# A fused retention and Fourier-mixing kernel: new turns for the work between batch 0's feed-forward products, and two filler matmuls moved to the head

## The chip, the cores and the metric

The kernel runs on one core of one Trainium2 chip. The metric is the device time of one execution in microseconds (us). Its engines are TensorE (PE in the profile; PEld is its loading of weights), VectorE (DVE), ScalarE (ACT), GpSimd (POOL) and SyncE (SP), which here only issues DMAs. Each works through its own queue in the order in which the program was written out for it.

## The reference, cut to what matters

Inputs are q, k and v of 4 batches, 8 heads, 768 positions and 64 channels, and two weights, w1 (512 x 2048) and w2 (2048 x 512). Per head, a decaying state is carried over the positions, then the heads are put side by side to x of 768 x 512 per batch:

```python
state = gamma * state + outer(k[t], v[t])
y[t] = (q[t] @ state) / sqrt(64)
```

Then x is mixed by a two-dimensional Fourier transform (over positions and channels) of which the real part is kept, added to itself, normalised per row, and sent through a feed-forward net:

```python
u = x + real(fft(fft(x, axis=1), axis=2))
un = (u - mean(u)) / sqrt(var(u) + 1e-6)
out = u + relu(un @ w1) @ w2
```

## The kernel before, in words

**Stages of a batch.** *Attention* goes by pairs of heads, four pairs a batch, in 6 chunks of 128 positions. `cast_unit` turns the loaded q, k and v into f16 on POOL (k scaled by powers of gamma), `t_unit` transposes q and k (batches 0 and 1 on PE, line 610, later ones by DMA), `a_unit` makes the products within a chunk (line 654) and masks them on DVE, `kv_unit` makes the states (line 673) and sums them over chunks on ACT and DVE, `y_unit` makes y from states and products (lines 704 and 708), which ACT scales into x (line 716). *Folding* (`fold_s`, `fold_d`, `fold_e`, DVE) uses the symmetries of the transform. *Stage one* (`s1_unit`, line 837) and *stage two* (`s2_unit`, from line 980) are the two transforms as products with tables. Stage two gives one block of 128 rows at a time: blocks 0 to 2 directly, blocks 3 to 5 as *mirror rows* from the reversed result of stage one. After the matmuls (lines 999, 1015, 1018) come copies on ACT, two sums on DVE, two sums with x on POOL (1027, 1029), statistics on DVE (1040, 1041), and on ACT `un`, the centred rows in f16 (1042). `unT_unit` transposes such a block (PE, line 1065, and a copy; from batch 1's block 3 on by DMA). The pool of `un` has two buffers. *Feed-forward*: the rows are in two halves of three blocks. The first product (`h_unit`, line 1078, 16 units of 4 matmuls; for batch 0's first half `h0_unit`, line 1095, 4 units of 16 small matmuls for each block) goes through relu on ACT or DVE (1082, 1084; 1102, 1104) into `ht16`. The second product (`ch_unit`, line 1121) takes a block of rows in four quarters of four matmuls; DVE adds u after the fourth (1125), and SP writes the block out (1129). PSUM, the matmuls' output memory, holds 5 buffers in the pool for attention and transforms, and 3 in the pool for the feed-forward.

**The head.** Batch 0's attention and transform are written out by hand in the text `FIRST`: each name is a unit, `@v`, `@a`, `@g` its engine, and `pin` fixes that order on every engine. It also has the eight weight loads `w0` to `w7` (POOL, lines 1135 and 1142), one each for a fourth of w1 and of w2. A *filler* is a 128x512 matmul of zeros (line 167) whose result is not used; `filler(6)()` at line 235 issues six before all else, and `fill1` in `FIRST` issues one.

**Turns.** After the head, everything is placed by due times. The feed-forward units of a batch are the *majors*: 56 units of batch 0 are due at 1/56, 2/56, ... 1.0. Here the 16th is a square root for the norm, the 17th to 28th are the quarters of the first half's second product, then 16 units of the first product of the second half, and so on. Every other list of units is a stream with a start and an end, and its units are due at even steps between them (`emit`, line 1238):

```python
for i, u in enumerate(units):
    ev.append((t0 + (t1 - t0) * (i + 1.0) / len(units), si, i, u))
ev.sort(key=lambda e: e[:3])
```

The units are written in that order. A scheduler at compile time then lays out each engine's queue: it takes earlier turns first, by its own estimates of durations, and lets a later turn go ahead where an earlier one has to wait for an operand or a buffer. On POOL, and for turns below 0.05 on every engine, the written order is fixed up to turn 1.0.

The constants for batch 0 and its border with batch 1 are: `DM0`, start and end of its mirror rows and of their transposes; `TS0`, start and end of batch 1's first cast and then the bounds of its five further steps of attention; `DA0`, counted from the end of `TS0`, start and end of batch 1's stage one, of its stage two for blocks 0 to 2, and of these blocks' transposes; `LD0`, the loads of batch 1, which wait for the seventh weight load (`w6`) and for the last first product of block 1; `HT0`, two units on DVE, `half_tables` (tables for stage two of batches 1 to 3) and `pad_unit` (zeros). `DM1`, `TS1`, `DA1` and `LD1` are the same for later batches.

Of the kernel before, what the change touches and what calls it, by code (L numbers as in the profile page):

```python
# [36 lines left out]
ae001@v kv0 ae000@v ae011@v t10 sc0 t11 e10@a yi01 v10@g yi00 yx0 e11@a am10 q2 x01@a am11 ts3  # L37
ta32 ta20 x00@v ta01 fl4@g ae101@v ae100@v k21@a kv1 t20 ta21 e20@a ae111@v yi11 t21 sc1
ae110@v yi10 fs0 fl2@g yx1 q3 s110 k31@g e21@a x10@v am20 am21 x11@a fs1 ta40 v22@a s010 k30@a
t30 e30@a fill1 t31 v21@g e31@a ae201@v ta30 ae200@v kv2 ae211@v yi21 ae210@v gk2@g sc2 csn2@a  # L40
w0 w1 csn1@v fill1 am30 ae300@v ta31 yi20 yx2 v32@g x20@a ae301@v xs0@v x21@a ta41 fl3@a gk3@g
s100 am31 ae311@v s000 v31@g kv3 fs2 s101 ge10@a ae310@v w2 s001 w3 yi31 sc3 ge00@a yi30 yx3 g0
x30@a sa00 sa10 edge x31@v fs3 w4 gr0 sa11 csn0@v s011 xs2@a xs3@v w5 s111 xs1@a sa20 mean
ge01@a sa02 sa01 ge11@v sa03 nh0@a gr3 sa12 nh1@a gr1 sa13 g1 sa21 pt0 g2 ua1@v pt1 sa22 pe0@a
# [1 line left out]
"""  # L46
ON_ACT = {'q': (0, 1, 0), 'kv': (1, 1, 1), 'g': (0, 1, 1), 'gr': (0, 0, 0)}
FB = 1
DM0, DM1 = (0.121, 0.179, 0.253, 0.368), (0.004, 0.137, 0.232, 0.341)
TS0 = (0.269, 0.376, 0.393, 0.441, 0.517, 0.575, 0.665, 0.696)  # L50
TS1 = (-0.040, -0.020, 0.048, 0.585)
DA0, DA1 = (0.034, 0.100, 0.173, 0.180, 0.306, 0.315), (0.063, 0.067, 0.063, 0.158, 0.168, 0.189)
LD0, LD1 = (0.160, 0.263), (-0.370, 0.140)
HT0 = (0.683, 0.767, 0.685, 0.583)
NPE = 2
ACT_ROWS = ((2, 5, 6, 7, 8, 9, 10, 14), (0, 3, 6, 7, 9, 10, 11, 12, 14, 15), (2, 4, 5, 6, 7, 8, 10, 14))

# [2 lines left out]
def kernel(  # L60
# [48 lines left out]
    gk2 = const.tile([P, NHP], f32, tag="gk2")  # L109
# [54 lines left out]
    def filler(n):  # L164
        def run():
            for _ in range(n):
                nc.tensor.matmul(wps, wz[:, 0:P], wz, start=True, stop=True)
        return run
# [63 lines left out]
    nc.gpsimd.iota(icol_i[:, 5:6], pattern=[[0, 1]], base=127, channel_multiplier=-1)  # L232
    nc.gpsimd.iota(kf_i, pattern=[[1, KN]], base=0, channel_multiplier=0)
    nc.gpsimd.memset(wz, 0.0)
    filler(6)()
    for h in range(H):
        nc.vector.memset(lgrow[:, h:h + 1], float(lng[h]))
    nc.vector.memset(maskf, 1.0)
# [1020 lines left out]
    for b in range(B):  # L1259
# [17 lines left out]
        if b + 1 < B:  # L1277
            steps = attn_steps(b + 1)
            if b == 0:
                streams.append(([load_unit(1, i, 6) for i in range(4)], LD0[0], LD0[1]))  # L1280
                streams.append(([qt_zeros], 0.1, 0.15))
                streams.append(([half_tables], HT0[0], HT0[1]))
                streams.append(([pad_unit], HT0[2], HT0[3]))
                ts = TS0
            else:
# [42 lines left out]
```

## Time and profile before

| what | us |
|---|---|
| time, median of 3 runs | 245.77 (245.33 to 245.82) |
| the profiled execution's own time | 246.28 |
| its span, first to last instruction | 244.1 |
| PE busy in the span | 231.0 |
| DVE busy | 173.6 |
| ACT busy | 121.3 |
| POOL busy | 83.5 |

The profile is of one execution. Its rows give starts in us from the span's start. A busy matmul row is longer than the time by which the next one follows, as matmuls overlap: a quarter's four 128x512 matmuls follow each other every 0.216 us, so that a quarter takes 0.86 us, and this is how the chain of waits counts them. In the chain, each row is what the next one waited for, in order of time; "issue" is time in which nothing that the profile shows was waited for. A row of the waits says: engine and line, who ended the wait, total us, how many waits. SPq and POOLq are the sequencers of SP and POOL, which issue DMAs. The batches' places in the span are: head to 33 us, batch 0's feed-forward from there to 94 us, then some 52 us for each of the others.

### The profile page before, as it was taken

What the parts mean: (1) busy time and instruction counts of PE and PEld (TensorE: products, weight loads), DVE (VectorE), ACT (ScalarE), POOL (GpSimd) and SP (SyncE); (2) the same over time, 40 slices, a digit from 0 to 9 for tenths busy, and PEclk for the clock granted to TensorE, in tenths of its full rate; (3) what the DMA queues carried; (4) which work ended last, traced back from release to release, by engine and by line L of the source; (5) the groups of instructions that cost most, each with busy time, mean ns of one, the idle gap of its engine ahead of it and who ended that gap; (6) DMA issues with size and microseconds to landing.
All of it is one profiled execution on the core that took longest, in us unless ns stands there. A gap on an engine that the chain in (4) does not pass through costs nothing.

```text
span 244.1 us, 5274 instructions
## 1 busy us (share of the span) xinstructions
PE 231.0 (95%) x2010; PEld 144.6 (59%) x2010; DVE 173.6 (71%) x423; ACT 121.3 (50%) x268; POOL 83.5 (34%) x151
## 2 busy tenths in 40 slices
PE   4499999997999998999999999999999999999995
PEld 1376779755775645665567446665666455445543
DVE  8879987947887788995985748887895556424112
ACT  5989758755785434842247515732257317202500
POOL 7578802456500067690000736660002305000000
PEclk9999999999999999999999999999999999999999
DMA  7997999999999388999999478585100441221012
GB/s 176 232 271 104 199 201 203 221 245 260 268 237 216 69 172 190 182 187 139 262 269 217 92 161 196 118 143 134 72 0 0 46 150 23 43 89 43 1 43 89
DMA packets 99209, 36.39 MB, mean 149 GB/s; under 512 B 89840, under 2 KB 96240, under 8 KB 99184
## 3 DMA queue, kind: packets, MB, share of 16 engines
q1 hardware_dynamic: 94960, 31.86, 63.2%
q0 software_dynamic: 4224, 4.19, 10.8%
q8 instruction: 16, 0.26, 0.5%
q14 instruction: 9, 0.07, 0.1%
HBM read 27.26 MB, written 6.29 MB: 137 GB/s over the span
## 4 chain that ended last, share of the span: by engine, by line
PE 79%; DVE 7%; ACT 4%; DMA 3%; POOL 3%; issue 1%; SPq 1%; POOLq 0%; ACTq 0%; DVEq 0%
PE psc L1121 34%; PE psh L1078 27%; PE wkA L654 3%; DMA v<-in_v_dram 3%; PE ps L837 3%; PE wkY L708 2%; PE pq L999 2%; PE wkY L704 1%; PE wkK L673 1%; PE tq L610 1%; PE ps L817 1%; SPq L209 1%; DVE bst L1040 1%; PE pq L911 1%; DVE atm L529 1%
## 5 line engine op out<-in xcount | busy, mean ns | idle before, releaser
L1121 PE MATMUL psc<-w,ht 128*128 128x512 f16 (+2 forms) x400 | 89.1, 370 | 0.1
L1078 PE MATMUL psh<-unT,w 128*128 128x384 f16 x448 | 81.9, 326 | 0.4 <-ACT ht L1082 0.2
L1121 PEld LDWEIGHTS <-ht 128*128 128x128 f16 x400 | 37.5, 98 | 36.8 <-issue 0.2
L1078 PEld LDWEIGHTS <-w 128*128 128x128 f16 x448 | 42.3, 98 | 24.6 <-issue 1.6
L1082 ACT ACTIVATE ht<-psh 128x384 f16<-128x384 f32 x64 | 30.9, 490 | 40.3 <-PE psh L1078 39.7
L1027 POOL TENSOR_TENSOR u<-u,x 128x256 f32<-128x256 f32 x21 | 13.3, 635 | 106.0 <-DVE u L1006 90.1
L1125 DVE SCALAR_TENSOR_TENSOR ob<-psc,stats,u 128x512 f32<-128x512 f32 (+2 forms) x25 | 18.1, 725 | 25.9 <-PE psc L1121 25.7
L1084 DVE TENSOR_SCALAR ht<-psh 128x384 f16<-128x384 f32 x48 | 26.1, 548 | 8.6 <-PE psh L1078 8.2
L657 DVE TENSOR_TENSOR atm<-wkA,maskp 128x512 f16<-128x512 f32 x36 | 23.9, 683 | 2.5 <-PE wkA L654 2.4
L1042 ACT ACTIVATE un<-u,stats 128x512 f16<-128x512 f32 x21 | 15.1, 721 | 17.9 <-DVE stats L1041 11.5
L683 DVE SCALAR_TENSOR_TENSOR s<-s,gk,wkK 128x128 f16<-128x128 f16 x48 | 16.2, 339 | 6.1 <-ACT s L679 5.5
L1040 DVE BATCH_NORM_STATS2 bst<-u 128x6 f32<-128x512 f32 x21 | 14.6, 694 | 8.3 <-POOL u L1029 8.1
L716 ACT ACTIVATE x<-wkY,gexp 128x384 f16<-128x384 f32 x24 | 12.8, 580 | 9.9 <-PE wkY L708 9.9
L431 POOL TENSOR_SCALAR kd<-k,gexp 128x384 f16<-128x384 f32 x24 | 13.8, 585 | 3.7 <-DMA k<-in_k_dram 2.8
L1029 POOL TENSOR_TENSOR u<-u,x 128x256 f32<-128x256 f32 x21 | 13.3, 635 | 2.4 <-DVE stats L1041 2.4
L654 PE MATMUL wkA<-qTz,kT 128*128 128x256 f16 x72 | 13.3, 273 | 0.1
L1095 PEld LDWEIGHTS <-w 128*128 128x128 f16 x192 | 11.0, 98 | 0.8 <-issue 0.3
L1095 PE MATMUL psh<-unT,w 128*128 128x128 f16 x192 | 11.4, 219 | 0.1
L1001 ACT COPY qn<-pq 128x128 f32<-128x128 f32 x18 | 4.9, 274 | 12.6 <-PE pq L999 11.9
L1006 DVE SCALAR_TENSOR_TENSOR u<-pq,g,qn 128x256 f32<-128x256 f32 x18 | 8.5, 472 | 3.1 <-PE psh L1078 2.5
L436 POOL TENSOR_SCALAR v<-v 128x768 f16<-128x768 f32 x12 | 10.0, 831 | 1.5 <-DMA v<-in_v_dram 1.5
L654 PEld LDWEIGHTS <-kT 128*128 128x128 f16 x72 | 6.9, 98 | 5.6 <-PE psh L1078 0.4
(177 smaller groups left out, 317.4 us busy)
## 6 DMA issues: line engine op xcount, KB each, us to landing
q<-in_q_dram SPq DMA_DIRECT2D x16, 384.0 KB, 6.0
k<-in_k_dram SPq DMA_DIRECT2D x16, 384.0 KB, 6.0
v<-in_v_dram SPq DMA_DIRECT2D x16, 384.0 KB, 6.1
out_dram<-ob SPq DMA_DIRECT2D x23, 256.0 KB, 2.4
w<-in_moe_w_ch_dram POOLq DMA_DIRECT2D x8, 512.0 KB, 11.6
unT<-un SPq DMA_TRANSPOSE x15, 2.4
out_dram<-ob SPq DMA_DIRECT2D x1, 192.0 KB, 1.9
qTz<-q16z SPq DMA_TRANSPOSE x8, 3.8
```

Source lines behind the costliest of these rows:

```text
L431: kc = nc.gpsimd.tensor_scalar(out=kd[:, :, h2, :], in0=k32[:, h2], scalar1=gkd[:, h0 + h2:h0 + h2 + 1], scalar2=1.0, op0=ALU.mult, op1=AL ...
L654: mm = nc.tensor.matmul(wk[:, c2], st["kT"][:, c, :], st["qT"][:, :, c, :], start=True, stop=True)
L657: nc.vector.tensor_tensor(out=st["atm"][:, 2 * part:2 * part + 2], in0=wk, in1=maskp[:, PAIR_ORDER[i]].unsqueeze(1).to_broadcast([P, 2, 2, ...
L683: nc.vector.scalar_tensor_tensor(out=s16[:, c], in0=s16[:, c - 1], scalar=gk2[:, hp:hp + 1], in1=wk[:, c - c0], op0=ALU.mult, op1=ALU.add)
L1040: nc.vector.bn_stats(bst, u[:, kb, :])
L1042: nc.scalar.activation(un, u[:, kb, :], AF.Identity, bias=stats[:, kb, 0:1], scale=-1.0)
L1078: nc.tensor.matmul(psh, w116[:, cb, fb * P:(fb + 1) * P], unT[:, cb, rt * 384:(rt + 1) * 384], start=(cb == 0), stop=(cb == 3))
L1082: nc.scalar.activation(ht16[:, fb, :], psh, AF.Relu, bias=0.0, scale=-1.0)
L1084: nc.vector.tensor_scalar(out=ht16[:, fb, :], in0=psh, scalar1=-1.0, scalar2=0.0, op0=ALU.mult, op1=ALU.max)
L1095: mm = nc.tensor.matmul(psh[:, f], w116[:, cb, fb * P:(fb + 1) * P], unT[:, cb, kb * P:(kb + 1) * P], start=(cb == 0), stop=(cb == 3))
L1121: nc.tensor.matmul(psc[:, c0:c1], ht16[:, fb, rb3 * P:(rb3 + 1) * P], w216[:, fb, c0:c1], start=(fb == 0), stop=(fb == NFB - 1))
L1125: nc.vector.scalar_tensor_tensor(out=ob[:, c0:c1], in0=psc[:, c0:c1], scalar=lb[b]["st"][:, rb, 3:4], in1=lb[b]["u"][:, rb, c0:c1], op0=AL ...
```

## The change

Two fillers leave `FIRST` and two join the six at the head. The constants for batch 0 and its border with batch 1 get other values; those of later batches stay, and no operation of the computation is added or taken out.

```diff
-t30 e30@a fill1 t31 v21@g e31@a ae201@v ta30 ae200@v kv2 ae211@v yi21 ae210@v gk2@g sc2 csn2@a
-w0 w1 csn1@v fill1 am30 ae300@v ta31 yi20 yx2 v32@g x20@a ae301@v xs0@v x21@a ta41 fl3@a gk3@g
+t30 e30@a t31 v21@g e31@a ae201@v ta30 ae200@v kv2 ae211@v yi21 ae210@v gk2@g sc2 csn2@a
+w0 w1 csn1@v am30 ae300@v ta31 yi20 yx2 v32@g x20@a ae301@v xs0@v x21@a ta41 fl3@a gk3@g
...
-DM0, DM1 = (0.121, 0.179, 0.253, 0.368), (0.004, 0.137, 0.232, 0.341)
-TS0 = (0.269, 0.376, 0.393, 0.441, 0.517, 0.575, 0.665, 0.696)
+DM0, DM1 = (0.161, 0.229, 0.218, 0.449), (0.004, 0.137, 0.232, 0.341)
+TS0 = (0.298, 0.379, 0.419, 0.451, 0.519, 0.575, 0.667, 0.685)
...
-DA0, DA1 = (0.034, 0.100, 0.173, 0.180, 0.306, 0.315), (0.063, 0.067, 0.063, 0.158, 0.168, 0.189)
-LD0, LD1 = (0.160, 0.263), (-0.370, 0.140)
-HT0 = (0.683, 0.767, 0.685, 0.583)
+DA0, DA1 = (0.110, 0.143, 0.161, 0.195, 0.290, 0.314), (0.063, 0.067, 0.063, 0.158, 0.168, 0.189)
+LD0, LD1 = (0.218, 0.221), (-0.370, 0.140)
+HT0 = (0.697, 0.821, 0.813, 0.608)
...
-    filler(6)()
+    filler(8)()
```

From these, the order of turns follows (by the rule of `emit`; "quarter n" is the n-th quarter of the first half's second product):

| work | due before | due after | stands before | stands after |
|---|---|---|---|---|
| mirror rows 3, 4, 5 of batch 0 | 0.140, 0.160, 0.179 | 0.184, 0.206, 0.229 | among block 1's first products | among block 2's |
| transposes of mirror row 5 | 0.368 | 0.449 | after quarter 5 | after quarter 10 |
| loads of batch 1, four pairs | 0.186 to 0.263 | 0.219 to 0.221 | spread over block 2's first products | together |
| batch 1's second cast | 0.401 | 0.424 | after quarter 7 | after quarter 8 |
| its second transposes | 0.417 | 0.435 | after quarter 8 | after quarter 9 |
| stage one of batch 1 | 0.746 to 0.796 | 0.803 to 0.828 | end of the second half's first product | from just ahead of quarter 1 of the second half to behind its quarter 2 |
| stage two of batch 1, blocks 0 to 2 | 0.871 to 0.876 | 0.857 to 0.880 | after quarters 4 and 5 of the second half | the same |
| transposes of its blocks 0 to 2 | 1.005 to 1.011 | 0.983 to 0.999 | after the last quarter | ahead of the last quarter |

## The prediction

> **What bounds the kernel now.** I read the page first, then the chain of waits, then the waits of TensorE, and then the timelines of single engines at the two places where the chain leaves TensorE after the head. Two lines of the page, engines and chain:
>
> ```profile
> PE 231.0 (95%) x2010; PEld 144.6 (59%) x2010; DVE 173.6 (71%) x423; ACT 121.3 (50%) x268; POOL 83.5 (34%) x151
> PE 79%; DVE 7%; ACT 4%; DMA 3%; POOL 3%; issue 1%; SPq 1%; POOLq 0%; ACTq 0%; DVEq 0%
> ```
>
> TensorE is the bound: work taken off DVE, ACT or POOL ends nothing sooner. What new turns can win is TensorE's idle time, and little is left. The waits of TensorE (total us, how many, longest):
>
> ```profile
> PE tq L610 <- POOL kd L431: 1.3, 1, 1.3
> PE pst L1065 <- ACT un L1042: 0.7, 1, 0.7
> PE psh L1078 <- ACT ht L1082: 0.2, 1, 0.2
> PE psh L1078 <- DVE ht L1084: 0.2, 1, 0.2
> ```
>
> All other waits of TensorE lie in the head, before 17 us. The first line's place, in the chain by time (start, length, what):
>
> ```profile
> 54.27 0.86 PE psc L1121 x4
> 55.14 0.35 PE tq L610 x6
> ...
> 55.59 1.16 POOL kd L431 x2
> ...
> 56.80 0.51 PE tq L610 x6
> ```
>
> Here TensorE has transposed q of batch 1's second head pair and stands until POOL has cast its k. POOL stood too, and SP's timeline says for what:
>
> ```profile
> 44.38 0.37 SPq L189 DMA_DIRECT2D q<-in_q_dram  x1
> 44.84 1.57 SPq L189 DMA_DIRECT2D k<-in_k_dram  x1
> 46.50 1.18 SPq L189 DMA_DIRECT2D v<-in_v_dram  x1
> 47.78 1.59 SPq L189 DMA_DIRECT2D q<-in_q_dram  x1
> 49.47 0.42 SPq L189 DMA_DIRECT2D k<-in_k_dram  x1
> ```
>
> The second k was issued at 49.47; the page's median from issue to landing is 6.0 us, so it lands at about 55.5, and the cast starts at 55.59. (The waits view gives POOL's stop to a transpose, which ended in the same tenth.) The first load started at 44.38 because it waits for weights, in SP's waits:
>
> ```profile
> SPq L189 <- DMA w<-in_moe_w_ch_dram: 27.5, 1, 27.5
> ```
>
> So 56.80 is set by a stream of DMAs, weights and then loads, and not by what TensorE did before. I call it the anchor. The second place is the border of batches 0 and 1:
>
> ```profile
> 89.87 2.59 PE psc L1121 x12
> 92.46 0.24 PE pst L1065 x4
> ...
> 92.81 0.73 ACT un L1042
> 93.54 0.05 issue
> 93.58 0.40 PE pst L1065 x4
> ```
>
> The third transposed row block waits for its normalised rows (un12), and these wait for the first block's transposes, whose buffer they take (two buffers).
>
> **The change, part by part.** The profiled execution took 246.28 us with a span of 244.1; the median of the three runs is 245.77, or 0.51 less. I sum differences, which hold against either, and give the time against the median.
>
> *Fillers.* Two move. At the head the six start 0.43 us apart from 2.15 us, so two more take 0.86 and end near 5.7; the next TensorE work starts at 6.11, where it waits for a cast. Cost 0, hidden in that wait. The two taken out ran at 21.07 and 22.41, and the next matmul began 0.33 and 0.41 later: at most 0.74 us off TensorE there. Whether TensorE reaches its fast spacing sooner with eight (transposes 0.107 us apart up to 13.8, 0.056 from 16.64) the trace can't show. For the end both are worth 0: whatever comes sooner or later by less than 1.3 us ahead of the anchor is taken up by the wait there.
>
> *Mirror rows of batch 0 (s2_unit 3 to 5).* Turns 0.140, 0.160, 0.179 become 0.184, 0.206, 0.229, behind all of the second row block's first product. In the trace their twelve matmuls ran at 37.36 to 39.06, ahead of that block's products, which waited for ACT (eight mask copies, 1.59 us, from 36.90, then the evictions at 38.49). A later turn does not shut them out: nothing else is ready in that gap, except the third block's four transposes. So I take 0; were the gap left empty, 1.48 us of them (1.70 less 0.22) would come later. On ACT and DVE the evictions go ahead of the mirror rows' copies and sums, which come perhaps 0.5 to 2 us later; their un03 was ready at 43.8 for transposes at 47.31, so that is covered. The third block's un05 is wanted last, after 58 us in the new order.
>
> *Loads of batch 1.* All twelve DMAs get their turn in one go; SP already held them in a row, behind the weights, with no other DMA between (the outputs follow at 61.50). They also wait for the second block's last first product, at about 42.7 (64 matmuls at 0.057 us from 39.02), 1.6 us ahead of the weights. Cost 0.
>
> *Turns of batch 1's attention.* Of the twelve quarters (0.86 us each) of batch 0's first second product, the second k transposes stand behind eight now and nine afterwards (turn 0.417 to 0.435; the ninth quarter's is 0.429). The last mirror row's transposes (0.22 us, 51.38 in the chain) move from ahead of them to behind (0.368 to 0.449). TensorE reaches the k transposes at 55.30 now; then 55.30 + 0.86 - 0.22 = 55.94, still ahead of 56.80. At the anchor it has done 0.64 us more: **-0.64**, and a wait of 0.86 stays. If the gap at 37.4 were empty, it would arrive at 57.42, 0.62 late, and -0.02 were left; that is the upper end. What is late next: the third pair's k cast ends at 60.8 (59.67 + 1.15) for transposes that move from 62.5 to 61.9, and the fourth's at 66.2 for 67.0 to 66.4. Both just hold, so the gain can't grow past about 0.8 here. The wkA products of the first pair come together behind the k transposes, its last one behind one quarter; the y products want it masked (0.69 us on DVE) 1.2 us later. Cost 0, at most 0.3. Pads and tables are DVE work without a hurry: 0.
>
> *Border of batches 0 and 1.* First stage products get turns 0.803 to 0.828 instead of 0.746 to 0.796; in the trace they ran at 81.13 to 84.0, already two quarters late, when their folds were ready. 0. The second stage keeps its slots. The three transposes go from behind the last quarter (1.005 to 1.011) to ahead of it (0.983 to 0.999). On the clock of before the first starts at 91.44, the second ends at 91.89. Statistics for un12 are there at 92.00 (91.82 + 0.18 on DVE), ACT first does a 0.30 us square root at 92.04, so un12 is ready at about 93.05. The wait is then 1.16 us less 0.216 for each of the last quarter's four matmuls that the scheduler puts ahead of the third transposes; it is 0.83 now (92.75 to 93.58). With all four: -0.53. With none: +0.33. The scheduler did cut quarters open for ready work at 81 us (one matmul, then six of stage one, then three), so I take between two and three: **-0.2**.
>
> The trace shows no wait of these transposes with work behind them that could run. The Trainium skill, "TensorE: Matmul & The Clock Gate", section "Step-by-step: what each phase is for", says that only weight loads are pulled ahead and matmuls stay in program order. By that rule, quarters written behind the third transposes wait with them (the +0.33 end, a sum of -0.31); were it not so, they would run in the wait (-0.53, a sum of -1.17).
>
> Sum: 0 + 0 + 0 - 0.64 - 0.2 = -0.84, so 245.77 - 0.84 = **244.9 us**.
>
> **Rivals.** (1) *The transposes stay together at the border.* -0.64 + 0.33 = -0.31: 245.5, no change. For it: in the trace the three stand in a row, though ten short matmuls behind them were ready in the 0.83 us wait. Against: a quarter's accumulator is already held, so it is easier to slip in. (2) *Mirror rows lose their gap.* -0.02 - 0.2: 245.5, no change. Against: the gap's cause, ACT, is untouched. (3) *Slower: un12 doesn't move with TensorE.* If stage two's chain (DVE, POOL and DVE in turn, from 85 to 92 us) ends when it does now, un12 is ready at 93.54, and what was won is waited away at the border, with a quarter still to do behind it: first products start at 93.58 + 0.22 + 0.86 = 94.66 instead of 94.50, with the ten short matmuls (0.68 us, 93.82 to 94.50) undone. +0.84: 246.6. It decides once un12 comes less than 0.84 earlier for an order without matmuls between. For it: POOL's two sums a row and DVE's statistics follow each other closely, with outputs (0.72 us at 90.35) between. Against: that chain starts from the folds, which wait for TensorE's y products. (4) *The whole border wait goes*: -1.17, 244.6.
>
> **How the numbers follow.** Three runs spread over 0.49 us, 0.2%, so 0.2% is about what can be told from no change. Forecast 0.47, rival 1 0.16, rival 2 0.10, rival 3 0.21, rival 4 0.06. Faster: forecast and rival 4, less 0.01 for its edge, 0.52. Same: rivals 1 and 2 and that 0.01, 0.27. Slower 0.21. The likeliest case's own range is 244.4 to 245.3. The whole range goes from 244.3 (rival 4 with 0.3 of scatter) to rival 3's 246.6; some 0.15 lies outside, mostly above.
>
> **What would show it.** In the changed profile: SP's first load of batch 1 still near 44.4; nine quarters before the second k transposes, these still at 56.8, TensorE's wait for kd down from 1.3 to about 0.7; mirror rows' matmuls still before 39; the third transposes at the border with one to four quarter matmuls between second and third, and a wait for un under 0.7. It is wrong if the first load starts later than 44.4 (each us there is a us at the end), if un waits grew beyond 1.2, or if a new TensorE wait stands between 57 and 67.

## The result, and the profile after

The changed kernel takes 246.15 us (median of 11 runs, 245.73 to 246.45), the kernel before 245.54 (11 runs beside it, 245.07 to 245.82). The ratio is 1.0022, with a 95% interval of 1.0013 to 1.0030: 0.6 us slower, where 244.9 was forecast. The profiled execution took 246.45 with a span of 244.2; that of before took 246.28 with 244.1, but it stood 0.5 to 0.7 above its kernel's medians, and this one 0.3. So the two traces look closer than the two kernels are, and the place where they differ most belongs to one execution, as the runs below show.

The page of the changed kernel, its engines and its chain:

```profile
PE 233.2 (96%) x2010; PEld 145.9 (60%) x2010; DVE 175.4 (72%) x423; ACT 121.8 (50%) x268; POOL 83.4 (34%) x151
PE 85%; DVE 4%; POOL 4%; DMA 3%; SPq 1%; issue 1%; ACT 1%; POOLq 0%
```

TensorE is busy 2.2 us more in a span of the same length. The waits of TensorE behind the head (total us, how many, longest):

```profile
PE psh L1078 <- DVE ht L1084: 0.3, 1, 0.3
PE pst L1065 <- ACT un L1042: 0.3, 1, 0.3
...
PE psh L1078 <- ACT ht L1082: 0.2, 1, 0.2
PE wkK L673 <- POOL v L436: 0.2, 1, 0.2
```

The 1.3 us for POOL's `kd` are gone, `un` costs 0.3 instead of 0.7, a wait for POOL's cast of v is new, and the one for DVE's `ht`, near 208 us, grew. TensorE's timeline at the anchor (start, length, what, idle time before it in brackets):

```profile
55.86 0.44 PE L673 MATMUL wkK<-v,kd 128*128 128x128 f16 x5
56.14 0.50 PE L610 MATMUL tq<-ident,q16z 128*128 128x128 f16 x6
56.47 0.50 PE L610 MATMUL tq<-ident,kd 128*128 128x128 f16 x6
```

It does not wait: the casts ran from 54.67 to 55.82, before TensorE was there. At the border of batches 0 and 1:

```profile
90.71 0.61 PE L1065 MATMUL pst<-ident,un 128*128 128x128 f16 x8
91.16 0.81 PE L1121 MATMUL psc<-w,ht 128*128 128x512 f16 x3
92.28 0.40 PE L1065 MATMUL pst<-ident,un 128*128 128x128 f16 x4 [0.31 <-ACT un L1042]
92.52 0.38 PE L1121 MATMUL psc<-w,ht 128*128 128x512 f16 x1
92.73 0.39 PE L999 MATMUL pq<-gk,g16r 128*128 128x129 f16 x4
93.28 0.27 PE L673 MATMUL wkK<-v,kd 128*128 128x128 f16 x2 [0.15 <-POOL v L436]
93.39 1.79 PE L1078 MATMUL psh<-unT,w 128*128 128x384 f16 x10
```

Three of the last quarter's matmuls run between the second and the third transposes, as forecast, and one behind. Two of batch 2's states (line 673) stand ahead of batch 1's first products and wait.

From 107.5 us on, every engine has the same order of operations in both kernels (TensorE already from 97 us, DVE from 100 us, POOL and SP everywhere). Yet the stretch near 203 us differs. DVE's timeline there, in the kernel before and in the changed one:

```profile
202.14 0.69 DVE L1040 BATCH_NORM_STATS2 bst<-u 128x6 f32<-128x512 f32 x1 [0.44 <-POOL u L1029]
202.87 0.18 DVE L1041 BATCH_NORM_AGGREGATE stats<-bst 128x2 f32<-128x6 f32 x1
202.97 0.47 DVE L1006 SCALAR_TENSOR_TENSOR u<-pq,g,qn 128x256 f32<-128x256 f32 x1
```

```profile
201.84 0.69 DVE L1040 BATCH_NORM_STATS2 bst<-u 128x6 f32<-128x512 f32 x1 [0.44 <-POOL u L1029]
202.56 0.18 DVE L1041 BATCH_NORM_AGGREGATE stats<-bst 128x2 f32<-128x6 f32 x1
203.01 0.48 DVE L1006 SCALAR_TENSOR_TENSOR u<-pq,g,qn 128x256 f32<-128x256 f32 x1 [0.27 <-PE psh L1078]
```

DVE was 0.31 us ahead, and then line 1006 started 0.45 instead of 0.10 behind the aggregate. The view puts this down to a product of the feed-forward, but line 1006 does not read it: it waits for a `pq` that had been finished at 201.7 and for ACT's copies, finished at 202.3, and the trace has its semaphore row as passed at 202.58. What hangs on it (POOL's sums, statistics, `ht`) is late by as much, and TensorE waits more at 208.

To compare executions, I count the 1040 feed-forward matmuls, whose order among themselves is the same in all kernels, and take the time between the starts of certain of them from each trace: A from number 0 to 256 (attention of batch 1 lies between), B from 320 to 416 (the border and the first product of batch 1), C from 832 to 864 (the last batch's mirror rows). "Full clock" is where the trace grants TensorE its full clock for good. All in us; "turns" says whose turns the attention has.

```
profile of                     turns   full clock  no. 0    A      B      C
before                         before  16.0        33.19   35.07  22.36  5.53
before, once more (e12)        before  15.9        33.15   34.03  22.36  5.53
fillers alone (e1)             before  21.3        33.92   33.81  22.36  5.53
border alone (e6)              before  21.1        34.06   33.80  22.56  5.53
before, a memset more (e7)     before  20.4        33.65   33.82  22.36  5.88
states later (e9)              before  16.2        33.09   34.83  23.25  5.53
whole quarter (e10)            before  16.1        33.04   33.99  22.27  5.52
changed                        after   20.9        33.80   33.74  22.56  5.89
turns alone (e2)               after   20.8        34.09   33.74  22.56  5.90
turns, eight at the head (e3)  after   20.4        33.70   33.80  22.56  5.88
turns, none later (e4)         after   20.4        33.52   33.75  22.59  5.88
border put back (e5)           after   15.5        32.94   33.75  22.36  5.88
changed, 3 memsets more (e8)   after   20.7        33.91   33.74  22.56  5.53
changed, states later (e11)    after   15.3        33.01   33.92  23.27  5.53
```

The other stretches agree within 0.03 us, but for 0.2 us from 416 to 832 in the changed kernel's own profile, which none of the runs with the same turns shows again.

### The profile page after: what moved, and what is told of

The parts are those of the page before. It is cut to its first block, busy times and chain, and to the rows that moved or that the text cites. A ratio compares the mean times of both kernels' runs of the same rounds, so it can differ in the third digit from the quotient of the medians.

```text
span 244.2 us, 5273 instructions
## 1 busy us (share of the span) xinstructions
PE 233.2 (96%) x2010; PEld 145.9 (60%) x2010; DVE 175.4 (72%) x423; ACT 121.8 (50%) x268; POOL 83.4 (34%) x151
## 4 chain that ended last, share of the span: by engine, by line
PE 85%; DVE 4%; POOL 4%; DMA 3%; SPq 1%; issue 1%; ACT 1%; POOLq 0%
PE psc L1121 31%; PE psh L1078 28%; PE psh L1095 3%; PE wkA L654 3%; DMA v<-in_v_dram 3%; PE ps L837 3%; PE ps L817 2%; PE wkY L708 2%; PE wkY L704 2%; PE pq L999 1%; PE wkK L673 1%; PE tq L489 1%; PE tq L610 1%; PE pq L911 1%; SPq L209 1%
```

## The experiments

Each kernel was timed beside the kernel before on the same chip: 245.65 us for the first four, 245.64 for the next four, 245.61 for the rest.

**Fillers or turns.** Two theories: A, moving the fillers costs what the turns win; B, the turns cost it. Four kernels take the change apart. Fillers of after, turns of before:

```diff
-t30 e30@a fill1 t31 v21@g e31@a ae201@v ...
-w0 w1 csn1@v fill1 am30 ...
+t30 e30@a t31 v21@g e31@a ae201@v ...
+w0 w1 csn1@v am30 ...
-    filler(6)()
+    filler(8)()
```

> Only the fillers moved (eight at the head, none later), the turns as before. Theory A, the fillers cost time in the head: the first product of block 0 starts up to 0.6 us later (33.80 instead of 33.19 in the changed kernel's profile), but TensorE waits for the second k of batch 1 behind it, so of the 0.6 us at most what exceeds that wait comes through: 0 to +0.2 us against before. Theory B, the new turns alone cost the 0.6 us: 0.0 us, and the first product at 33.2. If fillers cost without cover: +0.6 us.

Measured: 245.80 (12 runs), ratio 1.0005 (0.9989 to 1.0021). The time is theory B's, its first product is not: it starts at 33.92 instead of 33.2. That follows the clock and not the fillers, for with six fillers at the head the next run's starts at 34.09 (full clock at 21.3 and 20.8 us). Turns of after, fillers of before:

```diff
-DM0, DM1 = (0.121, 0.179, 0.253, 0.368), ...
-TS0 = (0.269, 0.376, 0.393, 0.441, 0.517, 0.575, 0.665, 0.696)
+DM0, DM1 = (0.161, 0.229, 0.218, 0.449), ...
+TS0 = (0.298, 0.379, 0.419, 0.451, 0.519, 0.575, 0.667, 0.685)
... (DA0, LD0 and HT0 of after as well)
```

> Only the turns changed, the fillers as before (six at the head, one and one later). Theory A, the turns gain what was forecast and the fillers take it away where there is no wait left to hide it: 0.3 to 0.8 us faster than before. Theory B, the new turns cost what the change costs: 0.6 us slower than before.

Measured: 246.27, ratio 1.0020 (1.0007 to 1.0032). The same turns with eight fillers at the head and the two later ones kept:

> New turns, eight fillers at the head and the two later ones kept. Theory A in the form that the two added ones are the cost (the clock's release comes later): +0.6 us against before, and the release near 20.9 us again. In the form that the two left out are the cost: as the turns alone, 0.3 to 0.8 us faster. Theory B: +0.6 us whatever the fillers.

Measured: 246.24, ratio 1.0021 (1.0009 to 1.0034). The same turns with six at the head and none later:

> New turns, six fillers at the head and none later. Theory A in the form that the two left out are the cost: +0.6 us against before, with the clock's release at its usual 16 us. In the form that the two added ones are the cost: 0.3 to 0.8 us faster than before. Theory B: +0.6 us whatever the fillers.

Measured: 246.34, ratio 1.0026 (1.0010 to 1.0041). B holds: the turns cost 0.6 us with any set of fillers, and the fillers nothing that can be measured.

**Border, or a place in DVE's program.** In the table, among the profiles with the later full clock, A is hardly shorter with the new turns, B is 0.20 longer and C 0.35. C was the riddle, as nothing there is in another order. One thing differed: DVE's program has 489 instructions instead of 488, since one instruction more needed a second semaphore, and the late line 1006 is the 448th that the trace records. The next four kernels test whether it is the place that costs (theory P) or the order (theory O). The border put back in the changed kernel:

```diff
-DA0, DA1 = (0.110, 0.143, 0.161, 0.195, 0.290, 0.314), ...
+DA0, DA1 = (0.110, 0.143, 0.161, 0.195, 0.317, 0.326), ...
```

> The changed kernel with the three transposes at the border of batches 0 and 1 put back behind the last quarter; all other new turns stay. Two theories of the 0.6 us that the new turns cost. Theory P (place, plus border): DVE's program has 489 instructions here, as in the changed kernel, against 488 before, and the instruction at its 448th place, line 1006 for batch 3's block 4 near 203 us, starts 0.35 us late with all that it waits for done; that costs 0.36 at the end, and the border's new order about 0.2. So P expects the stall to stay (line 1006 some 0.44 us behind its semaphore row instead of 0.09), and +0.3 (245.95 beside 245.65). Theory O (order): all 0.6 us comes from the new order at the border, and the late start near 203 us is a shift in phase that follows from it. O expects no stall, and -0.1 to 0.1 (245.55 to 245.75).

Measured: 245.88, ratio 1.0004 (0.9993 to 1.0015); B 22.36, C 5.88, line 1006 late. The time alone could not tell the theories apart; B and C do. The border alone in the kernel before:

```diff
-DA0, DA1 = (0.034, 0.100, 0.173, 0.180, 0.306, 0.315), ...
+DA0, DA1 = (0.034, 0.100, 0.173, 0.180, 0.279, 0.303), ...
```

> The kernel before with one edit: the three transposes at the border of batches 0 and 1 due ahead of the last quarter, as in the changed kernel. DVE's program keeps 488 instructions. Theory P: no late start near 203 us; the border alone gains 0.38 (third transposes) and gives back 0.22 and 0.37 in the two stretches of 32 matmuls behind it, so +0.2 (245.85 beside 245.65). Theory O: all that the new turns cost is in this edit, with the late start near 203 us: +0.6 (246.25). My forecast of the border, were it still right: -0.2.

Measured: 245.75, ratio 1.0010 (0.9998 to 1.0023); B 22.56, C 5.53, line 1006 in time. One memset more in the kernel before:

```diff
-    for h in range(H):
+    for h in list(range(1)) + list(range(H)):
         nc.vector.memset(lgrow[:, h:h + 1], float(lng[h]))
```

> The kernel before with one 128x1 memset more on DVE at the start, of a value that is set again right behind it: nothing else moves, and DVE's program has 489 instructions, so that line 1006 for batch 3's block 4 comes to its 448th place. Theory P: this line starts 0.35 us late near 203 us, the border is as before, +0.36 at the end (246.0 beside 245.65). Theory O: no late start, 0 (245.65).

Measured: 245.99, ratio 1.0014 (1.0000 to 1.0027). Its DVE, where every engine has the order of before:

```profile
201.37 0.69 DVE L1040 BATCH_NORM_STATS2 bst<-u 128x6 f32<-128x512 f32 x1 [0.44 <-POOL u L1029]
202.10 0.18 DVE L1041 BATCH_NORM_AGGREGATE stats<-bst 128x2 f32<-128x6 f32 x1
202.53 0.48 DVE L1006 SCALAR_TENSOR_TENSOR u<-pq,g,qn 128x256 f32<-128x256 f32 x1 [0.25 <-PE psh L1078]
```

The late start is there, as in the changed kernel. With three memsets more in the changed kernel, line 1040, which waits for POOL anyway, comes to that place:

```diff
-    for h in range(H):
+    for h in list(range(3)) + list(range(H)):
```

> The changed kernel with three such 128x1 memsets more on DVE at the start: DVE's program has 492 instructions, and to its 448th place comes line 1040 for the block ahead, which waits 0.44 us for POOL anyway. Theory P: no late start of line 1006, -0.36 against the changed kernel: 245.9 beside 246.25 for the changed kernel and 245.65 for the one before; the border's +0.2 stays. Theory O: as the changed kernel, +0.6 (246.25).

Measured: 245.79, ratio 1.0007 (0.9994 to 1.0020). Its DVE:

```profile
201.74 0.69 DVE L1040 BATCH_NORM_STATS2 bst<-u 128x6 f32<-128x512 f32 x1 [0.44 <-POOL u L1029]
202.47 0.18 DVE L1041 BATCH_NORM_AGGREGATE stats<-bst 128x2 f32<-128x6 f32 x1
202.56 0.47 DVE L1006 SCALAR_TENSOR_TENSOR u<-pq,g,qn 128x256 f32<-128x256 f32 x1
```

The late start is gone with all new turns kept. P holds, and it can be seen in C of every profile: 5.88 to 5.90 in the six with line 1006 at the 448th place, 5.52 or 5.53 in the eight others. In the kernel before, line 1009 has that place; it follows line 1006 at once, 0.38 us later on an engine still at work, and nothing shows.

**What the border gives back.** The border alone gains 0.36 us of idle time at the third transposes (from 0.84 to 0.47 between matmul starts, beyond their usual distance) and ends 0.20 worse over the 96 matmuls of B. DVE's rows around the wait, in the fillers' kernel (border of before) and then in the border's:

```profile
91.98 0.75 DVE L1125 SCALAR_TENSOR_TENSOR ob<-psc,stats,u 128x512 f32<-128x512 f32 x1
92.65 0.41 DVE L1067 COPY unT<-pst 128x512 f16<-128x512 f16 x1
93.50 0.42 DVE L1067 COPY unT<-pst 128x512 f16<-128x512 f16 x1 [0.43 <-PE pst L1065]
94.20 0.48 DVE L1006 SCALAR_TENSOR_TENSOR u<-pq,g,qn 128x256 f32<-128x256 f32 x1 [0.28 <-ACT qn L1002]
```

```profile
92.07 0.40 DVE L1067 COPY unT<-pst 128x512 f16<-128x512 f16 x1
93.05 0.42 DVE L1067 COPY unT<-pst 128x512 f16<-128x512 f16 x1 [0.58 <-PE pst L1065]
93.39 0.74 DVE L1125 SCALAR_TENSOR_TENSOR ob<-psc,stats,u 128x512 f32<-128x512 f32 x1
94.05 0.48 DVE L1006 SCALAR_TENSOR_TENSOR u<-pq,g,qn 128x256 f32<-128x256 f32 x1
```

The border's POOL and TensorE at the states:

```profile
92.72 0.83 POOL L436 TENSOR_SCALAR v<-v 128x768 f16<-128x768 f32 x1
...
93.61 0.27 PE L673 MATMUL wkK<-v,kd 128*128 128x128 f16 x2
```

And the third masks with the products that read them, first in the fillers' kernel, then in the border's:

```profile
102.32 0.68 DVE L657 TENSOR_TENSOR atm<-wkA,maskp 128x512 f16<-128x512 f32 x1
103.40 0.51 PE L708 MATMUL wkY<-v,atm 128*128 128x64 f16 x12
```

```profile
103.04 0.68 DVE L657 TENSOR_TENSOR atm<-wkA,maskp 128x512 f16<-128x512 f32 x1
103.46 0.73 PE L708 MATMUL wkY<-v,atm 128*128 128x64 f16 x12
```

Before, DVE's last add of batch 0 (`ob`, 0.75 us) ran while DVE waited for the third transposes anyway. With the quarter cut open its sum is complete only behind them, so the add stands ahead of batch 1's work. DVE's order changes behind it as well: line 1009 comes behind two relus instead of ahead of them (95.69 instead of 94.60), and POOL's next sum (line 1029) waits 1.00 us for it. The third masks then start at 103.04 instead of 102.32 (0.6 later, as this execution is 0.13 later as a whole at number 256), and TensorE idles 0.21 at line 708 for them and 0.08 at line 704, which it did not before. How much of that is the add and how much the relus was not taken apart. And TensorE reaches the states 0.3 us before v is cast: POOL's casts, which follow its last sum, did not move (they start at 90.51 and 90.64, the 0.13 by which the two executions differ), so 0.31 of what was won is waited away. Counted between matmul starts, gaps over 0.055 us from 90 to 106 us sum to 0.95 in the fillers' kernel (0.84 at the third transposes, 0.11 ahead of batch 1's first products) and to 1.12 in the border's (0.47 at the third transposes, 0.31 at the states, 0.08 at line 704, 0.21 at line 708, 0.06 at line 1078), which is 0.17 of the 0.20.

If the states were what eats the gain (theory G), moving them away would keep it. With the border's new order in the kernel before:

```diff
-DA0, DA1 = (0.034, 0.100, 0.173, 0.180, 0.306, 0.315), ...
+DA0, DA1 = (0.034, 0.100, 0.173, 0.180, 0.279, 0.303), ...
...
                 ts = list(TS1[:2]) + [TS1[2] + ... for j in range(6)]
+                if b == 1:
+                    ts[2] += 0.02
```

> The kernel before with the three transposes ahead of the last quarter, as in the run of the border alone, and with batch 2's first states (line 673) due 0.02 of a turn later, so that TensorE's queue has none of them between the third transposes and batch 1's first products. Theory G: of the border alone, the move itself gained (0.84 us idle at the third transposes became 0.48), and what ate it are the states pulled ahead, which wait 0.31 us for POOL's cast of v, and the masks on DVE that come later after them (0.18 at line 708). Then without the states ahead: -0.2 to -0.35 (245.3 to 245.45 beside 245.65), no TensorE wait for v line 436 at 93 us. DVE's 448th place holds line 1040, which waits anyway: no late start near 203 us. Theory H: what the move gains is lost behind it whatever the states do, since DVE and ACT hand over the same copies: 0 to +0.2 (245.65 to 245.85).

Measured: 246.57 (6 runs), ratio 1.0034 (1.0021 to 1.0048). Both theories fail. The edit moves more than the states: it moves the start of the whole step to which they belong, with the second pair's casts and transposes and the first pair's products within a chunk. The wait for v is gone and batch 1's products start 0.19 earlier than with the border alone (counted from number 320), but the first states come 3.3 us later, and so do their sums on DVE. The next pair's states then stand, by the view, for DVE's line 1009, which is queued among those sums:

```profile
102.02 0.33 PE L673 MATMUL wkK<-v,kd 128*128 128x128 f16 x3
102.98 0.29 PE L673 MATMUL wkK<-v,kd 128*128 128x128 f16 x2 [0.63 <-DVE u L1009]
103.15 0.81 PE L1078 MATMUL psh<-unT,w 128*128 128x384 f16 x4
```

Matmul starts are 0.79 further apart than usual there, and 0.38 once more at line 708: B is 0.89 longer than before. The same edit to `ts` in the changed kernel:

> The changed kernel with batch 2's first states due 0.02 of a turn later. DVE's program has 488 instructions, so line 1006 is not at the 448th place: no late start near 203 us. Theory G: both costs of the new turns are gone: -0.2 to -0.4 beside the kernel before (245.25 to 245.45). Theory H: 0 to +0.2 (245.65 to 245.85). My forecast for the whole change, were its sum right once these two costs are gone: -0.84.

Measured: 246.22 (11 runs), ratio 1.0029 (1.0019 to 1.0040); B 23.27, C 5.53. The late start is gone, and the states cost more than it did.

The other way keeps the quarter whole, between the second and the third transposes:

```diff
+DA0, DA1 = (0.034, 0.100, 0.173, 0.180, 0.285, 0.306), ...   (in the kernel before)
```

> The kernel before with the transposes at the border due at 0.987, 0.994 and 1.002 of the turns: the whole last quarter stands between the second and the third, and batch 2's states stay in one piece behind them, at the place of before. The third transposes should wait 0.26 us or less (0.48 less one matmul of 0.22; 0.84 before). Theory G: the states then still wait for v (cast until about 93.55) and hold the first products back, so about half of the gain stays: -0.1 to -0.3 (245.35 to 245.55). Theory H: 0 to +0.2.

Measured: 245.66, ratio 0.9995 (0.9985 to 1.0006); B 22.27, the shortest of all, 0.09 under before. The time is that of theory H, B is at the small end of theory G's gain, and the interval of the ratio (0.37 less to 0.15 more) can't tell 0.09 from nothing. Its DVE:

```profile
91.23 0.40 DVE L1067 COPY unT<-pst 128x512 f16<-128x512 f16 x1
91.72 0.75 DVE L1125 SCALAR_TENSOR_TENSOR ob<-psc,stats,u 128x512 f32<-128x512 f32 x1
92.39 0.41 DVE L1067 COPY unT<-pst 128x512 f16<-128x512 f16 x1
```

The add is back in the wait, and nothing shows up at line 708. The third transposes' idle time fell to 0.26, and the states' wait for v rose to 0.53: most of what is won at one is waited for at the other. So no version measured here is shown to beat the kernel before.

**The anchor.** The kernel before, once more:

> The kernel before, once more, for the wait that my forecast rested on. If the 1.3 us for which TensorE stood before the second k transposes in the first profile were usual, it is there again at 55 to 57 us. If it belongs to that one execution (a late stream of loads and an early head), then the second k has landed by 54.5 and TensorE, which reaches these transposes near 56, does not wait there.

Measured: 245.22 in one run. Its TensorE, and that of the fillers' kernel, whose turns are the same:

```profile
54.93 0.50 PE L610 MATMUL tq<-ident,q16z 128*128 128x128 f16 x6
55.71 0.51 PE L610 MATMUL tq<-ident,kd 128*128 128x128 f16 x6 [0.28 <-POOL kd L431]
```

```profile
55.72 0.50 PE L610 MATMUL tq<-ident,q16z 128*128 128x128 f16 x6
56.05 0.50 PE L610 MATMUL tq<-ident,kd 128*128 128x128 f16 x6
```

Neither of the two expectations came true as it stands: the wait is there, at a quarter of its size or less (0.28 where it was 1.33). Over the seven profiles with the attention turns of before, the idle time ahead of these transposes, counted between matmul starts, is 1.49, 1.23, 0.44, 0.41 and three times nothing. It needs an early TensorE: all four have the full clock from about 16 us and their first product by 33.2, while the three without it have the clock from 20.4 us or later and their first product at 33.65 or later. And its size follows the load: where 1.49 and 1.23 were lost, the second k landed at 55.4 and 55.1, in the other two at 54.3 and 54.2. None of the seven profiles with the new turns has this wait, two of them with an early clock among them.

## Why the prediction was wrong, point by point

*Fillers, 0.* Right: no set of them changed the time by more than its interval.

*Mirror rows and loads, 0.* The mechanism is right. In the changed profile the mirror rows' twelve matmuls fill the same gap, from 38.20 to 39.5, and the first load of batch 1 starts at 44.21, 0.17 earlier than before. The size is nearly right: ahead of the first quarter of the second product TensorE idles 0.19 to 0.21 us instead of 0.28 to 0.29, in every profile with the new turns (numbers 128 to 192 take 3.77 to 3.78 us instead of 3.85 to 3.86). DVE's order there changes with the mirror rows' sums; no run moved them alone, so that they are the cause is not shown. This gap lies in a stretch that the prediction left out: it speaks of two places where the chain leaves TensorE after the head, but the chain is off TensorE from 32.2 to 46.4 us too.

*Attention turns, -0.64.* This step failed. Of its mechanism this holds: with the new turns the wait is in no profile, and with the early clock A is 33.7 to 33.9, where it was 34.0 to 35.1 before. But the step took one profiled execution's wait, which the other profiles show to be the largest of seven, for the kernel's. With the later clock the wait is not there, and the step wins nothing: numbers 192 to 240, between which these transposes lie, take 15.33 to 15.34 us with the old turns (three profiles) and with the new ones (seven). In all ten TensorE idles some 0.22 us just behind the transposes instead (in the fillers' kernel at line 654, at 57.5 and 57.9), so that even a wait that goes does not give all of its length. The 0.06 by which A falls with the later clock (33.81 to 33.75) lies elsewhere: some 0.09 ahead of the first quarter, less 0.03 (in one profile 0.10) more ahead of the fourth pair's k transposes, whose cast the prediction had named as just holding. The signs were in the text: the execution was 0.51 above the median, and I noted it and summed "differences, which hold against either". A difference that ends in a wait does not.

*Border, -0.2.* The step's own mechanism came true: the scheduler cut the quarter, three matmuls went ahead, and the idle time went from 0.84 to 0.47, a gain of 0.36 where 0.21 was forecast. What failed is that the sum ended there. I asked what the third transposes wait for, and not what else used the wait: DVE's add of the last quarter did, and POOL's casts, which do not move with TensorE, stood 0.3 us behind it. The profile of before shows the cast:

```profile
93.11 0.83 POOL L436 TENSOR_SCALAR v<-v 128x768 f16<-128x768 f32 x1
...
94.05 0.44 PE L673 MATMUL wkK<-v,kd 128*128 128x128 f16 x5
```

Rival 1 read ten short matmuls as ready in the wait from 92.75 to 93.58; five of them are these states, and their v was ready at 93.94 only. (The prediction also says that no work that could run stood behind these transposes; it can't have both.) The border alone is +0.20 (B), not -0.2.

*The end of the sum.* It had no term for the last batch, since no turn there changes. The late start of DVE's line 1006 costs 0.35 (C), more than half of the result, and no term and no rival had it.

So the like-for-like sum is -0.06 + 0.20 + 0.35 = +0.49, against +0.6 measured (0.32 to 0.74 by the interval of the ratio). It also fits the others: +0.35 for the memset alone (measured +0.35), +0.20 for the border alone (+0.11), +0.14 for the changed kernel without the late start (+0.15), +0.29 with the border put back (+0.24), +0.89 for the states later (+0.96). It fits less well, but within the intervals, for the states later in the changed kernel (+0.85, measured +0.61) and for the whole quarter (-0.09, measured +0.05).

*Rivals.* The slower one, that un12 does not move with TensorE, is not what happened: in the border's kernel un12 starts at 91.85, with the old border at 92.28. It gave the right sign by a wrong mechanism, and the stated range holds 246.15 us only because of it: that was luck. Rival 1 (the transposes stay together) did not occur in the changed kernel, rival 2 (mirror rows lose their gap) neither. And none of the three signs of being wrong that the prediction names appeared: the first load was not later than 44.4, the wait for `un` did not exceed 1.2, and the waits view shows no new wait between 57 and 67 us. They watched the places that the sum already had; what was lost lies at 93, 103 and 203 us. One reading beside the point: a wait of 0.2 us in the head of before lies at 18.49, not before 17.

What stays open: why the 448th place starts late. In the eleven profiles in which the instruction there is not held up by another engine, a packet of 8,192 bytes of the kind "instruction" starts 0.65 to 0.70 us after it, so that a fetch of instructions lies nearby; that the one causes the other was not tested. The Trainium skill, "Runtime: NRT & Kernel Launch", section "Instruction fetch mechanics", says that engines take their instructions in 16 KiB blocks and that the cost of crossing a block is mostly hidden. The trace has packets of 16,384 bytes on one queue and of 8,192 on this one. If the late start is such a crossing, 0.35 us of it was not hidden; no run here shows that it is one.

## What to carry to other kernels

Before a wait is priced from a profile, ask what must coincide for it (here an early clock and a late load made the large one), and look for it in a second profile of the same kernel; the largest wait of one execution is the one most likely to be that execution's own. A wait that goes also takes away the room in which other engines did their work, so list what every engine does during it and where that will stand afterwards. Where two kernels differ at a place where their orders are equal, compare how many instructions each engine has: one instruction more can move a late start from a place where it is covered to one where it isn't.

## What the runs showed of the hardware that I had not expected

One memset of 128x1 on DVE at the start of the kernel before cost 0.35 us at 203 us (C 5.88 instead of 5.53), and three more in the changed kernel, whose DVE program has one instruction more by itself, took the same 0.35 away.

The full clock comes for good in one of two places, at 15.3 to 16.2 us (six profiles) or at 20.4 to 21.3 us (eight), in kernels with the same head too (16.1 in the whole quarter's, 21.1 in the border's), and with the first the feed-forward starts 0.3 to 1.2 us earlier. In four of the six profiles with eight fillers at the head it was granted once before, for 3.41 us from 5.0 to 7.0 us on, and then taken back for 6.83 or 10.24 us; in none of the eight with six fillers. That is few: the mean granted clock of these four profiles is 0.986 where 6.83 us were taken back and 0.979 where it was 10.24, and of the runs without a trace 0.986 stands beside six fillers too (13 of the 35 runs of the kernel before beside the first four experiments), 0.979 beside eight alone. The full clock came for good in the same two places, at 15.3 and 15.5 or at 20.4 and 20.7 us; whether the first two are sooner for the early grant (15.9 to 16.2 without it) two profiles can't tell. The Trainium skill, "TensorE: Matmul & The Clock Gate", section "What's actually happening", says that the clock goes by windows of 3.413 us that run freely, so that the moment differs from run to run; the stretches here (3.41, 6.83 and 10.24 us) are one, two and three of those windows, which agrees.
